# Five full query blocks and packed PV rows in a fused state-space and attention kernel

## The chip, the cores and the metric

The kernel runs on one core of a Trainium2 chip. The metric is device time in microseconds (us) of one execution. The span of a profile, from the first to the last instruction, is about 2 us shorter than the time of that execution. A single core is used, so there is one granted clock of TensorE. Some executions of the kernel before were slow for no reason that the kernel holds (1,502.79 and 804.85 us among the first). Ratios are the mean time of one kernel's fast runs over the mean of the other's fast runs of the same rounds, so they are not quite the ratio of the medians that I quote.

## The reference, cut to what matters

Two independent halves share the core, and their outputs stand side by side.

```python
# A: a diagonal complex state-space model, S = 2048 steps, D = 640 channels
h = Lam_bar * h + Bu[t]                      # a scan over time for each channel
y = 2 * Re(C h) + x * Dskip

# B: attention with 32 heads of Dh = 20, one key and one value head for all
q = (x @ wq)  -> 32 heads x 2048 x 20;  k = x @ wk (2048 x 20);  v = x @ wv (2048 x 20)
p = softmax(q k^T / sqrt(20))                # 32 x 2048 x 2048 exponentials
out = concat_heads(p v) @ wo                 # 640 x 640
```

The exponentials are the bulk: 2,048 tiles of 128 keys x 512 queries (4 query blocks x 32 heads x 16 key blocks).

## The kernel before

The kernel is a generator. A small scheduler in Python simulates the engines with a duration for each step, decides an order for each engine, and emits that order with semaphores. **So the order and the number of instructions of each engine are fixed before the chip starts.** What is left to the chip is how long each instruction takes and how long each engine waits at each semaphore. The steps that matter:

```python
CHUNKS = (3, 2)     # ScalarE takes score tiles in chunks of 3 and 2: 1,536 and 1,024 columns of PSUM
NPS = 7             # buffers (PR) that hold the exponentials until the PV matmuls have read them
NDS = 18            # buffers (DR) of the tiles whose exponential VectorE and GpSimd make with integer steps

def fill(self, op, i):                      # score matmuls of one chunk, then its exponential
    ...
    ex = self.act(lambda e: e.activation(dst, t[:, 0:512 * n], ACT.Exp, scale=1.0 / UNIT), ...,
                  gate=lambda: not h.taken or (h.left == 0 and self.s.done(h.users)))
                  # h: a PR buffer. It is free when all PV matmuls that read it are done
```

A head has 20 rows, and this kernel lets each head start at a multiple of 32 partitions. So four heads are padded to 4 x 32 = 128 partitions, and 32 heads need eight groups. Queries are made in that padded form with 32 matmul columns for 20 useful ones. So are PV, the normalisation and the output projection:

```python
self.WO4 = sb(o, "WO4", [128, NGG, 640], BF16)    # NGG = 8 padded groups
self.OT  = self.sb(s, "OT", [128, 10, 512], BF16) # normalised PV, padded
self.rdB = sb(o, "rdB", [128, 2, 512], BF16)

def queries(self, qb, gg, bank, prev, deps, whole):        # 8 groups x 5 chunks x 4 quarters a query block
    for c in range(NC):                                    # NC = 5
        for j in range(4):
            lhs = p.wqf[:, 640*c + 80*gg + 20*j : ... + 32]
            fns.append(self.mm(bank.tensor[32*j:32*j+32, ...], lhs, p.xbT[:, c, 512*qb:512*qb+512], ...))

def normalize(self, b, ev):                                # after the PV result of head group b is in pvsb
    # denominators to DRAM and back as 64 x 32, reciprocal, to DRAM, then read back on all rows of rdB by DMA
    self.norm_op[b] = self.dve(self.tt(p.OT[:, ot, :], p.pvsb[:, slot, :], p.rdB[:, slot, :], ALU.mult), ...)

def o_task(self, qb, k, bank):
    for gg in range(NGG):                                  # 8 steps of accumulation
        ... self.mm(out, p.OT[:, ots[gg], 128*ts:128*ts+128], p.WO4[:, gg, ...], ...)
```

At the head of the program, sine and cosine tables are made: GpSimd and VectorE reduce the angles, ScalarE applies the sine, then it loads the exponential's table. The first attention exponential comes after that.

Of the kernel before, what the change touches and what calls it, by code (L numbers as in the profile page):

```python
# [402 lines left out]
LIFT = 40.0 * UNIT  # L403


class Build:
    CHUNKS = (3, 2)
    MISC = 2
    NPS = 7
# [17 lines left out]
    def build(self):  # L427
        nc = self.nc
        with ExitStack() as o:
# [22 lines left out]
            with ExitStack() as p2:  # L452
                self.alloc_late(p2)
                late = base - nc.sbuf_bytes_remaining
                if late < early:
                    self.sb(p2, "pad", [128, (early - late) // 4 + 8], FP32)
                self.program()
                self.s.run()
                shares = {k: self.EARLY for k in self.LATE}
                shares.update({f"W{c}_1": [f"xbT{i}_{k}" for i in range(2) for k in range(NC)] for c in range(NC)})  # L460
                shares.update({k: ["xn0", "xn1"] for k in ("CT0", "CT1")})
                em = Emitter(nc, self.s.order, [b.key for b in self.banks], shares)
                em.plan()
                with nc.Block() as block:
                    em.emit(block)

    def alloc(self, o):
# [16 lines left out]
        self.WO4 = sb(o, "WO4", [128, NGG, 640], BF16)  # L484
# [7 lines left out]
        self.aq = sb(o, "aq", [128, 4, 512], BF16)  # L492
# [4 lines left out]
        self.Mm = sb(o, "Mm", [128, NGG, 32], BF16)  # L497
# [9 lines left out]
        self.rdB = sb(o, "rdB", [128, 2, 512], BF16)  # L507
# [9 lines left out]
    def alloc_early(self, s):  # L517
        self.maskM = self.sb(s, "maskM", [128, NGG, 32], FP32)
# [5 lines left out]
        self.EARLY = ["iota", "early_fr00", "early_fr01", "early_fr10", "early_fr11", "vrow", "maskM", "ones32", "mask0"]  # L524

    def alloc_late(self, s):
        self.W = self.sb(s, "W", [128, NC, 2, 512], BF16)
        self.g = self.sb(s, "g", [128, 2, 2, 512], BF16)
        self.OT = self.sb(s, "OT", [128, 10, 512], BF16)
        self.LATE = [f"W{c}_0" for c in range(NC)] + [f"g{u}_{i}" for u in range(2) for i in range(2)] \  # L530
            + [f"OT{i}" for i in range(10)]
# [67 lines left out]
    def program(self):  # L599
# [4 lines left out]
        self.qt_op, self.row_op = {}, {}  # L604
        self.vp_op, self.kt_op, self.vs_op = {}, {}, {}
        self.tasks = []
        self.evac_op, self.norm_op, self.spread_op = {}, {}, {}
        self.o_ops, self.y_ops, self.w_op, self.xa_op = {}, {}, {}, {}
# [63 lines left out]
    def constants(self):  # L672
# [14 lines left out]
        def select(t, pattern, op, v, base, mult, dur):  # L687
# [14 lines left out]
        many("mask0", [fill(p.mask0[:], -1.02, 200),  # L702
# [4 lines left out]
        many("maskM", [fill(p.maskM[:], -1.02, 300),  # L707
                       select(p.maskM[:], [[1, 8], [0, 4], [-1, 8]], ALU.is_equal, 0.0, 0, 0, 650),
                       select(p.maskM[:], [[0, 8], [-32, 4], [0, 8]], ALU.is_ge, 0.0, 0, 1, 650),
                       select(p.maskM[:], [[0, 8], [32, 4], [0, 8]], ALU.is_ge, 0.0, 19, -1, 650)])  # L710
# [10 lines left out]
        self.c_op["WO4"] = self.dve(lambda e: e.memset(p.WO4[:], 0.0), 1500, writes=["WO4"], prio=2.5,  # L721
                                    gate=lambda: self.tile_n > 128)
# [3 lines left out]
    def loads(self):  # L726
# [13 lines left out]
        for c in range(NC):  # L740
# [6 lines left out]
        o = self.loadT([(p.xaT[:, c, :], xa[0, 0:1024, 128 * c:128 * c + 128]) for c in range(NC)], 780000, "xa0", issue=1930.0,  # L747
                       writes=["xaT0", "xaT1"])
        self.xa_op[0] = self.xa_op[1] = o
        self.bt_op = [self.loadT([(p.BT[:, ri, cd, :], src[:, 128 * cd:128 * cd + 128]) for cd in range(NC)], 819200,  # L750
                                 f"bt{ri}", writes=[f"BT{ri}"]) for ri, src in ((0, self.B_re), (1, self.B_im))]
        self.ct_op = [self.loadT([(p.CT[:, ri, cd, :], src[:, 128 * cd:128 * cd + 128]) for cd in range(NC)], 819200,
                                 f"ct{ri}", writes=[f"CT{ri}"]) for ri, src in ((0, self.C_re), (1, self.C_im))]
        wov = self.wo.rearrange("(gg jr) n -> jr gg n", jr=80)
        fns = [lambda e, j=j: e.dma_start(p.WO4[32 * j:32 * j + 20, :, :], wov[20 * j:20 * j + 20, :, :])
               for j in range(4)]
        self.wo_op = self.dma(fns, 819200, "wo", reads=["WO4"], writes=["WO4"], deps=[self.c_op["WO4"]])
# [5 lines left out]
    def xa_load(self, tb):  # L763
        p = self
        self.xa_op[tb] = self.loadT([(p.xaT[:, c, 512 * (tb % 2):512 * (tb % 2) + 512],
                                      self.A_x[0, 512 * tb:512 * tb + 512, 128 * c:128 * c + 128]) for c in range(NC)],
                                    655360, f"xa{tb}", writes=[f"xaT{tb % 2}"])
# [7 lines left out]
    def kv_steps(self):  # L775
# [65 lines left out]
        def bound():  # L841
# [6 lines left out]
            self.mm_op = self.dve(self.ts(p.Mm[:], p.maskM[:], p.mab[:, 4:5], None, ALU.mult), 250,  # L848
                                  deps=[m, self.c_op["maskM"]], reads=["mabs", "maskM"], writes=["Mm"], prio=0.5)
# [67 lines left out]
    def qt_task(self, qb, gg, bank):  # L917
        p = self
        prev = None
        slot = (8 * qb + gg) % 12  # L920
        prev = self.queries(qb, gg, bank, None, [self.wqa_op if gg == 0 else self.wq_op] + bank.last, True)
        dst = p.QT[:, slot, :]
        key = f"QT{slot}"
        first = (qb, gg) == (0, 0)
        if first:
            ev = self.act(lambda e: e.activation(dst, bank.ap, ACT.Copy), 600, deps=[prev], reads=[bank.key],
                          writes=[key], prio=0.3)
        else:
            ev = self.dve(lambda e: e.tensor_copy(dst, bank.ap), 600, deps=[prev], reads=[bank.key], writes=[key],  # L929
                          prio=self.EV)  # L930
        aq = self.dve(self.ts(p.aq[:, gg % 4, :].bitcast(I16), dst.bitcast(I16), 0x7FFF, None, ALU.bitwise_and), 270,
                      deps=[ev], reads=[key], port=True,
                      writes=[f"aq{gg % 4}"], prio=0.4 if first else 2, gate=lambda: self.aq_free(qb, gg))
        self.qt_op[(qb, gg)] = (ev, aq)
        if qb == 0 and gg == 0:
            prev = self.queries(qb, gg, bank, prev, [ev, self.wq0_op], False)
            yield lambda: self.mm_op is not None
            m = self.pe([self.mm(bank.tensor[32 * j:32 * j + 32, bank.off:bank.off + 512], p.M0[:, j, :], p.aq[:, 0, :], False,
                                 True, tile_position=(0, 32 * j), skip_group_check=True) for j in range(4)], self.mmt(512),
                        deps=[self.m0_op, aq], prev=prev, prio=0.5, mode="C", reads=["M0", "aq0", key],  # L940
                        writes=[bank.key])
            ev = self.dve(self.ts(dst, bank.ap, p.lift[:, 0:1], p.lift[:, 1:2], ALU.add, ALU.min), 720,
                          deps=[m, self.lift_op], reads=[bank.key, "lift"], writes=[key, "QTr0"], prio=0.4)
            self.row_op[(0, -1)] = ev
# [4 lines left out]
    def aq_free(self, qb, gg):  # L949
        n = qb * NGG + gg  # L950
        if n < 4:
            return True
        w = self.row_mm.get((n // 4) - 1)
        return w is not None and self.s.done([w])

    row_mm = {}

    def row_task(self, qb, half, bank):
        p = self
        ggs = range(4 * half, 4 * half + 4)  # L960
        prev = None
        rs = (2 * qb + half) % 2
        deps = [self.mm_op] + [self.qt_op[(qb, gg)][1] for gg in ggs] + bank.last
        for gg in ggs:
            prev = self.pe([self.mm(bank.tensor[0:32, bank.off:bank.off + 512], p.Mm[:, gg, :], p.aq[:, gg % 4, :],
                                    gg == ggs[0], gg == ggs[-1])], self.mmt(512), load=128.0, deps=deps, prev=prev,
                           prio=1.5, reads=["Mm", f"aq{gg % 4}"], writes=[bank.key])
        self.row_mm[2 * qb + half] = prev
        ev = self.dve(self.ts(p.brow[:, rs, :], bank.tensor[0:32, bank.off:bank.off + 512], LIFT, 0.0, ALU.add,
                              ALU.min), 620, deps=[prev], reads=[bank.key], writes=[f"brow{rs}"], prio=0.7)  # L970
        lo, ng = 4 * half, 4
        if qb == 0 and half == 0:
            lo, ng = 1, 3
        at = (8 * qb + lo) % 12
        fns = [lambda e, j=j: e.dma_start(p.QT[32 * j + 20:32 * j + 21, at:at + ng, :],
                                          p.brow[8 * j + lo:8 * j + lo + ng, rs, :]) for j in range(4)]
        self.row_op[(qb, half)] = self.dma(fns, 32768, f"row{rs}",
                                           deps=[ev] + [self.qt_op[(qb, gg)][0] for gg in ggs],
                                           reads=[f"brow{rs}"] + [f"QT{i}" for i in range(at, at + ng)],
                                           writes=[f"QTr{i}" for i in range(at, at + ng)], prio=0, land=500.0)  # L980
# [5 lines left out]
    def block_ready(self, b):  # L986
        qb, gg = divmod(b, NGG)
        return self.row_key(b) in self.row_op and (qb, gg) in self.qt_op

    @staticmethod  # L990
    def row_key(b):
# [902 lines left out]
```

## Time and profile before

| | value |
|---|---|
| fast runs, first rounds | 783.91 and 781.43 us; later rounds had medians of 782.2 to 783.2 us |
| span | 781.1 us |
| first exponential starts | 25.6 us (head) |
| last exponential ends | 769.46 us, so the stream is 743.8 us long |
| exponentials busy / ScalarE idle inside the stream | 735.0 / 8.8 us |
| from there to the end | 11.6 us (tail) |

The span is head + busy + idle + tail: 25.6 + 735.0 + 8.8 + 11.6 = 781.1 (rounded terms).

First the page's head (part 1): the span, then busy time, share of the span and instruction count of each engine.

```profile
span 781.1 us, 24633 instructions
...
PE 733.0 (94%) x10668; PEld 247.9 (32%) x10668; DVE 667.5 (85%) x1228; ACT 751.6 (96%) x674; POOL 439.2 (56%) x451
...
```

ScalarE (ACT) is at 96%, TensorE (PE) at 94%. The Trainium skill, "Perfetto Trace Analysis", section "Identifying the Most-Contended Engine", says that busy time is a fair measure of how close ScalarE is to its limit, and that matmul busy time is not one for TensorE.

Next the groups of instructions, by shape. After the names come the count, then busy us in total, mean ns of one, then idle time just before them and what ended it. (Means overlap, so busy is less than count times mean.)

```profile
...
L1079 ACT ACTIVATE PR<-SC 128x1536 bf16<-128x1536 f32 x324 | 505.8, 1561 | 8.0 <-PE MB L581 4.2 <-PE SC L581 3.5
...
L1079 ACT ACTIVATE PR<-SC 128x1024 bf16<-128x1024 f32 x324 | 369.1, 1139 | 2.4 <-PE MB L581 2.4
L596 DVE TENSOR_SCALAR DR<-MB 128x512 int16<-128x512 f32 x428 | 285.4, 684 | 61.5 <-PE MB L581 56.7
...
L581 PE MATMUL MB<-xbT,wqf 128*32 128x512 bf16 x640 | 46.5, 385 | 1.3 <-DVE xbT L797 0.6 <-ACT xbT L800 0.5 <-DVE DR L596 0.2
...
L577 PE MATMUL MB<-WO,OT 128*32 128x512 bf16 x416 | 30.9, 381 | 0.0
...
L577 PE MATMUL MB<-WO,OT 128*32 128x128 bf16 x512 | 11.0, 220 | 0.0
...
L577 PE MATMUL SC<-WO,OT 128*32 128x512 bf16 x96 | 5.8, 379 | 0.0
...
```

The first two lines are the stream: 324 pairs, and their busy times together, counted without overlap, are 735.0 us on the page, so 2.27 us a pair. The third line is the 428 tiles that VectorE takes in place of ScalarE. The last four are what the change reduces: queries (46.5 us) and output projection (30.9 + 11.0 + 5.8 = 47.7 us).

The timeline of ScalarE (start us, duration us, what, count; idle before it in brackets), first and last rows of the stream:

```profile
...
25.62 2.37 ACT L1079 ACTIVATE PR<-SC 128x1536 bf16<-128x1536 f32 x2 [1.55 <-PE SC L581]
...
754.68 14.78 ACT L1079 ACTIVATE PR<-SC 128x1024 bf16<-128x1024 f32 x13
...
```

25.62 is where the stream starts, 754.68 + 14.78 = 769.46 where it ends. What ScalarE's exponentials waited for (us in total, times, longest):

```profile
...
ACT PR L1079 <- PE MB L581: 6.5, 7, 1.5
...
ACT PR L1079 <- PE SC L581: 3.5, 4, 1.5
...
```

The second of these is a wait for scores (SC); the first is a wait for PV matmuls (MB, the PV bank) to finish. 1.55 us of the scores' wait is before the first exponential.

### The profile page before, as it was taken

Reading aid. Unit: us, or ns where it says so; the run is one execution under the profiler, and the core shown is the slowest. Engines: PE = TensorE matmul, PEld = TensorE weight load, DVE = VectorE, ACT = ScalarE, POOL = GpSimd, SP = SyncE. Lnnn points to the kernel's source line nnn. Section 1 sums busy time; section 2 is a strip of 40 time slices with the busy share of each in tenths; the row PEclk is TensorE's granted clock in tenths of the full one; section 3 lists DMA queues with packets and bytes.
Section 4 is the critical chain, followed back from the end, with each engine's and each line's share of the span. In section 5 each row is a group of like instructions: output and inputs, shape, how many; then the busy total and the mean of one; then the engine's idle time right before and its main releaser. Section 6 shows DMA issues by size and latency. Waiting matters only on the chain.

```text
span 781.1 us, 24633 instructions
## 1 busy us (share of the span) xinstructions
PE 733.0 (94%) x10668; PEld 247.9 (32%) x10668; DVE 667.5 (85%) x1228; ACT 751.6 (96%) x674; POOL 439.2 (56%) x451
## 2 busy tenths in 40 slices
PE   8998999999999899999998999999899999999998
PEld 3322222222233333322322332323222333233324
DVE  7899898889988888899998787898889888885985
ACT  5899999999999999999999999999999999999994
POOL 3365655535556445664246645657665575676771
PEclk9999999999999999999999999999999999999999
DMA  9850100000000000011000000110000000001001
GB/s 195 131 96 22 38 9 5 8 8 9 9 9 9 24 16 22 23 25 33 17 16 9 24 30 17 29 30 17 9 11 8 23 30 15 22 11 33 12 9 43
DMA packets 54187, 21.61 MB, mean 28 GB/s; under 512 B 43464, under 2 KB 54080, under 8 KB 54080
## 3 DMA queue, kind: packets, MB, share of 16 engines
q1 hardware_dynamic: 52748, 19.90, 11.8%
q8 instruction: 84, 1.38, 0.7%
q10 hardware_dynamic: 1332, 0.15, 0.1%
q14 instruction: 23, 0.19, 0.1%
HBM read 7.20 MB, written 5.50 MB: 16 GB/s over the span
## 4 chain that ended last, share of the span: by engine, by line
ACT 76%; PE 18%; DVE 3%; POOL 1%; DMA 1%; issue 1%; ACTq 0%; POOLq 0%; DVEq 0%
ACT PR L1079 75%; PE MB L581 7%; PE SC L581 6%; PE MB L577 5%; DVE DR L596 1%; DMA wqf<-in_B_wq_dram 1%; POOL DR L591 1%; PE SC L577 1%; DVE prod L591 0%; DVE WO L721 0%; DVE pvsb L1348 0%; DVE prod L595 0%; DVE Z L1590 0%; DVE Z L1597 0%; DVE QT L929 0%
## 5 line engine op out<-in xcount | busy, mean ns | idle before, releaser
L1079 ACT ACTIVATE PR<-SC 128x1536 bf16<-128x1536 f32 (+1 forms) x648 | 735.0, 1350 | 10.4 <-PE MB L581 6.5
L591 POOL TENSOR_TENSOR DR<-DR,step 128x512 int32<-128x512 int32 x414 | 424.1, 1046 | 308.5 <-DVE DR L596 129.7
L596 DVE TENSOR_SCALAR DR<-MB 128x512 int16<-128x512 f32 x428 | 285.4, 684 | 61.5 <-PE MB L581 56.7
L581 PE MATMUL SC<-QT,KT 32*128 32x512 bf16 x1620 | 252.7, 384 | 35.1 <-ACT PR L1079 25.7
L581 PE MATMUL MB<-DR,VS 128*32 128x512 bf16 x1712 | 233.9, 386 | 3.0 <-DVE pvsb L1348 1.1
L581 PE MATMUL MB<-PR,VP 128*32 128x512 bf16 x1620 | 218.9, 385 | 0.9 <-ACT PR L1079 0.5
L581 PE MATMUL MB<-QT,KT 32*128 32x512 bf16 x428 | 156.5, 385 | 0.9 <-DVE DR L596 0.6
L581 PEld LDWEIGHTS SC<-QT,KT 32*128 32x128 bf16 x1620 | 64.2, 91 | 265.6 <-ACT PR L1079 168.4
L596 DVE TENSOR_SCALAR DR<-DR 128x1024 int16<-128x1024 int16 (+1 forms) x248 | 92.7, 425 | 6.5 <-PE MB L581 4.5
L581 PEld LDWEIGHTS MB<-DR,VS 128*32 128x32 bf16 x1712 | 57.5, 94 | 69.5 <-issue 37.0
L581 PEld LDWEIGHTS MB<-PR,VP 128*32 128x32 bf16 x1620 | 55.1, 94 | 63.7 <-issue 45.8
L577 PE MATMUL MB<-xaT,BT 128*32 128x512 bf16 x800 | 59.3, 382 | 0.0
L591 DVE TENSOR_TENSOR prod<-MB,Z 128x1024 bf16<-128x1024 f32 x40 | 48.7, 1216 | 7.7 <-PE MB L577 7.4
L581 PE MATMUL MB<-xbT,wqf 128*32 128x512 bf16 x640 | 46.5, 385 | 1.3 <-DVE xbT L797 0.6
L581 PE MATMUL MB<-KT,VZ 128*32 128x256 bf16 x844 | 43.7, 275 | 0.0
L581 PEld LDWEIGHTS MB<-QT,KT 32*128 32x128 bf16 x428 | 36.7, 91 | 20.3 <-issue 11.7
L577 PE MATMUL MB<-WO,OT 128*32 128x128 bf16 (+1 forms) x928 | 40.6, 292 | 0.0
L1652 DVE TENSOR_TENSOR_SCAN g<-sc,hst,u 128x512 bf16<-128x512 f32 x30 | 40.4, 1348 | 0.0
L591 DVE TENSOR_TENSOR prod<-g,tab 128x1024 bf16<-128x1024 bf16 x40 | 34.9, 872 | 0.0
L1469 DVE CAST stg<-MB 128x512 bf16<-128x512 f32 x35 | 24.0, 687 | 9.2 <-PE MB L577 8.9
L577 PE MATMUL MB<-CT,W 128*32 128x512 bf16 (+1 forms) x640 | 29.0, 300 | 1.5 <-issue 1.5
L577 PE MATMUL MB<-CT,xbT 128*32 128x512 bf16 (+1 forms) x640 | 29.4, 300 | 0.0
(126 smaller groups left out, 391.7 us busy)
## 6 DMA issues: line engine op xcount, KB each, us to landing
out_dram<-stg SPq DMA_DIRECT2D x35, 128.0 KB, 1.8
rdB<-recs SPq DMA_DIRECT2D x124, 32.0 KB, 1.8
CT<-in_B_x_dram SPq DMA_DIRECT2D x2, 640.0 KB, 5.8
WO<-in_B_wo_dram SPq DMA_DIRECT2D x4, 200.0 KB
wqf<-in_B_wq_dram SPq DMA_DIRECT2D x1, 680.0 KB, 5.2
out_dram<-PR SPq DMA_DIRECT2D x5, 128.0 KB, 1.8
sums<-pvsb SPq DMA_DIRECT2D x31, 4.0 KB
dn<-sums SPq DMA_DIRECT2D x31, 4.0 KB, 1.8
```

What stands on the lines that cost most here:

```text
L577: r = e.matmul(out[32 * j:32 * j + 32], lhsT=lhsT[:, 32 * j:32 * j + 32], rhs=rhs, start=start, stop=stop, tile_position=(0, 32 * j), skip ...
L581: return lambda e: e.matmul(out, lhsT=lhsT, rhs=rhs, start=start, stop=stop, **kw)
L591: return lambda e: e.tensor_tensor(out, a, b, op)
L596: return lambda e: e.tensor_scalar(out, a, s1, s2, op0=op0, op1=op1)
L1079: ex = self.act(lambda e: e.activation(dst, t[:, 0:512 * n], ACT.Exp, scale=1.0 / UNIT), 0.8333 * 512 * n + 64, table="exp", deps=[op], re ...
L1469: ev = self.dve(lambda e: e.tensor_copy(st, bank.ap), 620, deps=[prev], reads=[bank.key], writes=[key], prio=self.EV, gate=(lambda: last.e ...
L1652: o = self.dve(lambda e, ri=ri, init=init: e.tensor_tensor_scan(p.g[:, u, ri, :], rdec, p.u[:, ri, :], init, ALU.mult, ALU.add), 1280, por ...
```

## The change

Intent: do not pad where padding is not needed. Queries are made as five full blocks of 128 rows, written to DRAM, and read back into the padded rows by DMA. PV results are sent by DMA from padded to packed rows; the reciprocal is spread by DMA in the packed form too; normalisation and projection then need five blocks instead of eight groups. That frees TensorE and VectorE and costs DMA issues. The core of the diff:

```diff
-    NPS = 7
+    NPS = 8
+    NOP = 7
+    NRD = 3
...
-        self.WO4 = sb(o, "WO4", [128, NGG, 640], BF16)
+        self.WO = sb(o, "WO", [128, NC, 640], BF16)
+        self.WOt = sb(o, "WOt", [128, 640], BF16)
-        self.aq = sb(o, "aq", [128, 4, 512], BF16)
+        self.QP = sb(o, "QP", [128, NC, 512], BF16)
-        self.rdB = sb(o, "rdB", [128, 2, 512], BF16)
+        self.rdP = sb(o, "rdP", [128, self.NRD, 512], BF16)
-        self.OT = self.sb(s, "OT", [128, 10, 512], BF16)
+        self.OP = self.sb(s, "OP", [128, self.NOP, 512], BF16)
...                                               # the padding rows of the query tile, once, in the head
+        many("QTz", [("pool", lambda e, i=i: e.memset(p.QT[:, i:i + 2, :], 0.0), 600) for i in (1, 3, 5, 7, 9)]
+             + [("pool", lambda e: e.memset(p.QT[:, 11, :], 0.0), 330)], "QTz")
...                                               # queries: a full block, out to DRAM
+    def q_task(self, qb, blk, bank):
+        for c in range(NC):
+            at = 640 * c + 128 * blk
+            prev = self.pe([self.mm(bank.ap, p.wqf[:, at:at + 128], p.xbT[:, c, 512 * qb:512 * qb + 512], ...)])
+        ev = self.dve(lambda e: e.tensor_copy(dst, bank.ap), 600, ...)
+        out = self.dma(lambda e: e.dma_start(rows, dst), 131072, f"qd{blk}", deps=[ev], ...)
...                                               # and back into the heads' padded rows
+            fns = [lambda e, ...: e.dma_start(p.QT[32 * j:32 * j + 20, at:at + ng, :], q[j][:, lo:lo + ng, :])
+                   for j in range(4)]
...                                               # PV result to packed rows, reciprocal likewise, then one multiply
+            fns = [lambda e, ...: e.dma_start(p.OP[to:to + n, at, :], p.pvsb[32 * j + d:32 * j + d + n, slot, :])
+                   for j, d, to, n in parts]
+            fns = [lambda e, ...: e.dma_start(p.rdP[to:to + n, rd, :], recs[j:j + 1, :].to_broadcast([n, 512]))
+                   for j, d, to, n in parts]
+                    self.tt(p.OP[0:rows, at, :], p.OP[0:rows, at, :], p.rdP[0:rows, rd, :], ALU.mult), 350, ...
...                                               # projection: five steps (six for the last query block)
+        for blk in range(NC):
+            steps.append((NC * qb + blk, p.OP[:, at, :], p.WO[:, blk, :], [f"OP{at}", "WO"]))
+        if last:
+            steps.append((NC * NQB, p.pvsb[:, slot, :], p.WOt[:], [f"pvsb{slot}", "WOt"]))
```

Cut: the bound on the scores (a row that keeps the exponential in range) is computed for full blocks as well; loads of one half are issued in smaller pieces. Bytes a partition, by the shapes above: 2,560 less in the weights, 3,072 less in the PV results, 1,024 more for the reciprocals (4,608 less), and 3,072 more for an eighth buffer for exponentials, 3 x 512 columns of bf16.

## The prediction

> **What bounds it now.** The span is 781.1 us. ScalarE is the pace: the page gives it 96% busy, and the chain of waits runs through its exponentials for 75%. Groups by shape: 324 exponentials of 1,536 and 324 of 1,024 columns, 735.0 us together, so 2.27 us a pair (0.454 us a score tile), with 10.4 us idle before them, part of it at the start. The timeline has the first at 25.6 us and the last ending at about 769.5: 25.6 head + 735 + 9 idle + 11.6 tail. The other 428 of 2,048 score tiles get their exponential on VectorE; TensorE is 94% busy, VectorE 85%, the DMA engines nearly idle after 60 us.
>
> **What the change does**, from instruction counts of both programs:
> - TensorE: query matmuls 640 to 420 (46.5 us before, so about -16), output projection 1,024 to 672 (47.7, about -16), bound rows 32 to 20 (-3.6): 36 us freed.
> - VectorE: query evictions 31 to 20 (0.684 us each), absolute values 32 to 21 (0.30), normalisations 32 to 21 (0.49), bound-row evictions 8 to 4, no 2.2 us memset: 21 us freed.
> - DMA issues on the sync queue 341 to 550 at about 0.5 us: some 105 us more of a queue that mostly waits.
> - Six more GpSimd memsets before the start.
>
> **How much is critical.** Freed TensorE and VectorE time does not shorten ScalarE's stream; only fewer tiles on ScalarE do. The program moves just 15: exponentials on VectorE 428 to 443, ScalarE's 648 to 642. That is 3 pairs, 6.8 us. Most freed time is spent again: 15 first evictions (10 us), more shifted copies (about 11), 60 more PV matmuls (8). ScalarE's stream goes from 735.0 to about 728.2 us.
>
> Head: VectorE range-reduction steps now stand behind the third max-reduction, and memsets between GpSimd's table steps; I expect the first exponential 1 us later (26.6). The second head block waits for query and bound rows by DMA after 55 ScalarE tiles, at 51 to 52 us. By durations of before, evictions, absolute values and bound row end near 47; then query rows and bound rows are issued, landing near 51 to 52. I expect a stall of 0 to 3 us there, 1 in the middle. Later query blocks come hundreds of tiles ahead. The Trainium skill, "DMA: Bandwidth & Descriptors", "Rules for kernel authors", says to issue a DMA early and wait late, so that its fixed cost overlaps; this trace's 1.8 us to landing agrees with a cost that can hide. In-order coupling of sync queue and VectorE (absolute values in place wait for the query write): 2 us more idle.
>
> Tail: the last projection has six steps instead of eight, about -1 us.
>
> Sum: 26.6 + 728.2 + 9 + 1 + 2 + 10.7 = 777.5 us span; with the 2 us between span and time, 779.5. Against the fast time of before, 783.91, that is -0.6%: within 2%. (The median 804.85 holds slow runs.) Range 770 to 797; chances 0.14 faster, 0.79 same, 0.07 slower.
>
> **What shows it.** Exponentials about 728 us; the first at 26 to 27.5 us; query and projection matmuls about 30 us each; ScalarE's idle 10 to 15 us, the largest gap near 51 us, for query rows; DMA share under 0.2 after 60 us; tail 10 to 11 us.
>
> **What would make it wrong.** The in-order sync queue holding scatters or query reads behind a wait, so that evictions and then ScalarE stall in every block (slower). Or freed TensorE time removing most of ScalarE's idle (a few us faster). Over 2% faster needs nearly no idle: 26 + 728 + 10 is 764 already.

## More of the kernel before

Last a detail of the head, from VectorE's timeline. It looked harmless: five small steps of 128 x 5 elements.

```profile
...
12.50 0.99 DVE L595 TENSOR_SCALAR trig<-sc 128x5 f32<-128x5 f32 x5 [0.23 <-POOL fr L596]
...
```

They take 0.99 us together.

## The result, and the profile after

Four runs of the changed kernel gave 771.84 to 774.01 us, median 772.62. The ratio to before is 0.9874, 95% interval 0.9838 to 0.9909. A second set (below) gave the same median and 0.9863 (0.984 to 0.9886). So it is faster by 1.3 to 1.4%, which is within 2%. It lies inside the predicted range, but the predicted gain was 0.6%. Page, groups, timeline and waits, in the order of before:

```profile
span 770.8 us, 23905 instructions
...
PE 718.7 (93%) x10155; PEld 240.9 (31%) x10158; DVE 668.6 (87%) x1235; ACT 743.6 (96%) x668; POOL 438.8 (57%) x453
...
```

```profile
...
L1142 ACT ACTIVATE PR<-SC 128x1536 bf16<-128x1536 f32 x321 | 510.5, 1590 | 3.8 <-PE MB L587 1.9 <-PE SC L587 1.8
...
L1142 ACT ACTIVATE PR<-SC 128x1024 bf16<-128x1024 f32 x321 | 375.4, 1169 | 0.4 <-PE MB L587 0.2 <-PE SC L587 0.2
L602 DVE TENSOR_SCALAR DR<-MB 128x512 int16<-128x512 f32 x443 | 294.5, 684 | 60.1 <-PE MB L587 54.8 <-POOL DR L597 0.2
...
L583 PE MATMUL MB<-xbT,wqf 128*32 128x512 bf16 x400 | 28.7, 390 | 0.0
...
L583 PE MATMUL MB<-WO,OP 128*32 128x512 bf16 x260 | 20.8, 382 | 0.0
...
L583 PE MATMUL MB<-WO,OP 128*32 128x128 bf16 x320 | 6.8, 220 | 0.0
...
L583 PE MATMUL SC<-WO,OP 128*32 128x512 bf16 x60 | 4.3, 379 | 0.0
...
```

```profile
...
29.43 4.75 ACT L1142 ACTIVATE PR<-SC 128x1536 bf16<-128x1536 f32 x4 [0.55 <-PE SC L587]
35.42 19.75 ACT L1142 ACTIVATE PR<-SC 128x1536 bf16<-128x1536 f32 x17 [1.24 <-PE SC L587]
55.35 5.54 ACT L1142 ACTIVATE PR<-SC 128x1024 bf16<-128x1024 f32 x5 [0.17 <-PE SC L587]
...
743.96 16.06 ACT L1142 ACTIVATE PR<-SC 128x1536 bf16<-128x1536 f32 x14
...
```

```profile
...
ACT PR L1142 <- PE MB L587: 2.0, 4, 1.5
ACT PR L1142 <- PE SC L587: 2.0, 3, 1.2
...
```

TensorE's work fell as counted: queries 46.5 to 28.7 us (this line has 400 of 420), projection 47.7 to 20.8 + 6.8 + 4.3 = 31.9, and 1.8 more in 32 matmuls of the last query block's sixth step. VectorE took 443 tiles instead of 428 and is as busy as before (668.6 against 667.5). The stream has 321 pairs. It starts at 29.43 us and ends at 743.96 + 16.06 = 760.02. ScalarE's waits for PV fell from 6.5 to 2.0 us.

| term, us | before | predicted | after | change |
|---|---|---|---|---|
| head | 25.6 | 26.6 | 29.4 | +3.8 |
| exponentials busy (648 / 642 / 642) | 735.0 | 728.2 | 726.9 | -8.1 |
| ScalarE idle in the stream | 8.8 | 12 | 3.7 | -5.1 |
| tail | 11.6 | 10.7 | 10.8 | -0.9 |
| span | 781.1 | 777.5 | 770.8 | -10.3 |

Two terms were mis-sized, in opposite directions: the head and the idle. The head first. In VectorE's timeline of the changed kernel, the small steps are small no more:

```profile
...
7.64 1.69 DVE L602 TENSOR_SCALAR sc<-sc 128x5 f32<-128x5 f32 x1
...
14.10 3.10 DVE L601 TENSOR_SCALAR trig<-sc 128x5 f32<-128x5 f32 x4 [0.24 <-POOL fr L602]
...
20.38 0.16 DVE L597 TENSOR_TENSOR sc<-sc,trig 128x5 f32<-128x5 f32 x1 [1.08 <-POOL fr L602]
20.58 0.68 DVE L601 TENSOR_SCALAR sc<-sc 128x5 f32<-128x5 f32 x1
...
```

Four of the five 128 x 5 steps now take 3.10 us. In GpSimd's timeline of the same time:

```profile
...
7.47 0.94 POOL L694 TENSOR_SCALAR_AFFINE_SELECT pick<-pick 20x640 f32<-20x640 f32 x1 [2.98 <-DVE sc L1597]
8.36 0.94 POOL L718 MEMSET QT<- 128x1024 bf16 x1
...
14.01 2.97 POOL L718 MEMSET QT<- 128x1024 bf16 x3
...
20.29 0.95 POOL L718 MEMSET QT<- 128x1024 bf16 x1
...
```

Three memsets of the query tile run from 14.01 to 16.98 us, just while three of those steps crawl, about one memset long each. The earlier step at 7.64 us (1.69 us) overlaps the mask step and the first memset in the same way. Under the memset at 20.29 us a two-input step (`tensor_tensor`) still took 0.16 us, and the one-input `tensor_scalar` step after it 0.68 us. So it is the `tensor_scalar` steps that suffer. The Trainium skill has this: "SBUF — State Buffer", section "Who interferes with whom", says that GpSimd and VectorE's two-port modes share one pair of ports, that it is an exclusive lock held for the whole instruction, and that `tensor_scalar` can enter those modes. I had not carried it over to steps of five elements.

Last the windows view of the changed kernel: length, then busy us and instructions of each engine (PE, PEld, DVE, ACT, POOL), then granted clock, DMA share and GB/s.

```profile
...
28.00:52.00 24.00, 23.03 (x322) 9.02 (x326) 21.00 (x49) 22.09 (x21) 11.84 (x19) 0.86 0.46 95
52.00:100.00 48.00, 45.38 (x593) 14.64 (x595) 43.67 (x81) 47.83 (x43) 28.44 (x29) 1.00 0.36 78
100.00:200.00 100.00, 91.62 (x1127) 28.46 (x1119) 91.47 (x170) 100.00 (x90) 55.36 (x55) 1.00 0.07 19
...
```

The DMA engines are not idle after 60 us, as I had said: their share is 0.36 from 52 to 100 us (0.39 from 60 to 100), where it was 0.18 before; from 100 us on it is about 0.1. No wait of ScalarE can be read from it; the only idle near the start of the second head block is the 0.17 us at 55.35 us in the timeline above. The clock of 0.86 in the first row is a stretch of 6.8 us at half clock, from 28.7 us on; see the next section.

### The profile page after: what moved, and what is told of

It reads as the page before. It is cut to its first block, busy times and chain, and to the rows that moved or that the text cites. A ratio compares the mean times of both kernels' runs of the same rounds, so it can differ in the third digit from the quotient of the medians.

```text
span 770.8 us, 23905 instructions
## 1 busy us (share of the span) xinstructions
PE 718.7 (93%) x10155; PEld 240.9 (31%) x10158; DVE 668.6 (87%) x1235; ACT 743.6 (96%) x668; POOL 438.8 (57%) x453
## 4 chain that ended last, share of the span: by engine, by line
ACT 82%; PE 13%; DVE 3%; DMA 1%; POOL 0%; issue 0%; ACTq 0%; SPq 0%; POOLq 0%
ACT PR L1142 82%; PE MB L583 5%; PE MB L587 4%; PE SC L587 4%; DMA wkr<-in_B_wk_dram 1%; PE SC L583 1%; DVE DR L602 1%; DVE trig L601 0%; POOL fr L602 0%; DMA xaT<-in_A_x_dram 0%; DVE fr L602 0%; ACT tab L1647 0%; DVE sc L602 0%; PE MB L936 0%; DVE sc L1597 0%
## 5 line engine op out<-in xcount | busy, mean ns | idle before, releaser
L1142 ACT ACTIVATE PR<-SC 128x1536 bf16<-128x1536 f32 (+1 forms) x642 | 726.9, 1380 | 4.3 <-PE MB L587 2.0
L597 POOL TENSOR_TENSOR DR<-DR,step 128x512 int32<-128x512 int32 x410 | 418.3, 1044 | 301.3 <-DVE DR L602 128.5
L602 DVE TENSOR_SCALAR DR<-MB 128x512 int16<-128x512 f32 x443 | 294.5, 684 | 60.1 <-PE MB L587 54.8
L587 PE MATMUL MB<-DR,VS 128*32 128x512 bf16 x1772 | 225.9, 385 | 0.7 <-DVE DR L602 0.3
L587 PE MATMUL MB<-QT,KT 32*128 32x512 bf16 x443 | 162.8, 384 | 0.6 <-DVE DR L602 0.4
L602 DVE TENSOR_SCALAR DR<-DR 128x1024 int16<-128x1024 int16 (+1 forms) x275 | 101.6, 423 | 6.6 <-PE MB L587 4.8
L587 PE MATMUL MB<-KT,VZ 128*32 128x256 bf16 x860 | 45.5, 275 | 0.0
L1750 DVE TENSOR_TENSOR_SCAN g<-sc,hst,u 128x512 bf16<-128x512 f32 x30 | 42.3, 1415 | 0.0
L583 PE MATMUL MB<-xbT,wqf 128*32 128x512 bf16 x400 | 28.7, 390 | 0.0
L583 PE MATMUL MB<-WO,OP 128*32 128x128 bf16 (+1 forms) x580 | 27.1, 292 | 0.0
```

The source lines that it names most:

```text
L583: r = e.matmul(out[32 * j:32 * j + 32], lhsT=lhsT[:, 32 * j:32 * j + 32], rhs=rhs, start=start, stop=stop, tile_position=(0, 32 * j), skip ...
L587: return lambda e: e.matmul(out, lhsT=lhsT, rhs=rhs, start=start, stop=stop, **kw)
L597: return lambda e: e.tensor_tensor(out, a, b, op)
L602: return lambda e: e.tensor_scalar(out, a, s1, s2, op0=op0, op1=op1)
L1750: o = self.dve(lambda e, ri=ri, init=init: e.tensor_tensor_scan(p.g[:, u, ri, :], rdec, p.u[:, ri, :], init, ALU.mult, ALU.add), 1280, por ...
```

## The experiments

Every build goes through the scheduler again, so a small edit reorders the whole program. The count of exponentials is known before the run. Idle and tail still move by a microsecond or two from order alone, and I do not read differences of that size as effects. Fast medians of the kernel before in e1 to e4, e5 to e8, e9 to e11 and e12 were 782.8, 782.9, 782.2 and 783.2 us.

| run | exponentials | head | busy | idle | tail | span | median time | ratio to before |
|---|---|---|---|---|---|---|---|---|
| before | 648 | 25.6 | 735.0 | 8.8 | 11.6 | 781.1 | 782.8 | |
| after | 642 | 29.4 | 726.9 | 3.7 | 10.8 | 770.8 | 772.6 | 0.9874 |
| e1 late memsets | 643 | 24.8 | 728.7 | 3.8 | 11.5 | 768.8 | 770.9 | 0.9852 |
| e2 seven buffers | 643 | 29.5 | 728.1 | 5.8 | 11.6 | 774.9 | 776.3 | 0.9928 |
| e3 query half, seven buffers | 645 | 29.3 | 730.9 | 5.5 | 11.9 | 777.5 | 780.2 | 0.9968 |
| e4 output half, seven buffers | 646 | 25.4 | 731.7 | 9.2 | 11.2 | 777.5 | 779.1 | 0.995 |
| e5 before + memsets | 648 | 29.5 | 734.8 | 7.2 | 11.7 | 783.2 | 785.5 | 1.0042 |
| e6 after, 428 tiles on VectorE | 648 | 29.4 | 733.5 | 4.1 | 10.4 | 777.4 | 779.9 | 0.9974 |
| e7 output half, eight buffers | 646 | 25.8 | 730.6 | 3.7 | 10.0 | 770.2 | 771.1 | 0.985 |
| e8 late memsets, margin 500 | 640 | 24.9 | 725.8 | 8.0 | 11.2 | 769.8 | 773.4 | 0.9887 |
| e9 before, eight buffers | 650 | 25.6 | 737.3 | 6.8 | 11.9 | 781.6 | 781.7 | 0.9986 |
| e10 late memsets, ahead 8 | 642 | 25.2 | 727.2 | 6.7 | 12.9 | 772.0 | 773.9 | 0.989 |
| e11 e8 with nine buffers | 643 | 24.8 | 728.2 | 3.5 | 13.0 | 769.4 | 770.8 | 0.9851 |
| e12 after, unaltered | 642 | 28.9 | 726.8 | 4.4 | 10.8 | 771.0 | 772.6 | 0.9863 |

Head, idle and tail are read as for before and after: first and last exponential from ScalarE's timeline, busy from the groups. The terms come from rounded rows and can be 0.1 us off. (e7, e8, e10 and e11 have one more exponential than was counted ahead, for a single left-over tile.) The rows "after" and e12 are one program on two occasions: 0.5 us of head and 0.7 us of idle lie between them.

**One thing besides the order seems to move the idle: the clock.** In every profile the granted TensorE clock falls to half for one or more stretches (of 3.4, 6.8 or 10.2 us where they begin before the stream ends), and some of ScalarE's gaps fall into them. Before: 76.4 to 79.8 us, with 1.1 of its 8.8 us of idle in it or just after it. e4: 502.5 to 505.9 us (`prof e4_o_only --windows 502.5:505.9` gives a clock of 0.50), with a single gap of 2.3 us. e9: 29.6 to 33.0 and 149.1 to 152.5 us, with 2.6 us. e10: among others 512.4 to 515.8 us, with 1.5 us. e7 has none inside the stream. Most of the others have theirs in the first microseconds of the stream, where a gap can also come from the order. Times go with it: the four runs of e8 took 771.5, 771.8, 775.0 and 777.2 us at mean clocks of 0.997, 0.997, 0.991 and 0.984. Why the clock falls, and why elsewhere in another order, no run shows; nor does any run fix the clock, so that a gap comes from it is argued from place and time. So idle is compared below with these stretches in mind, and times at equal clock where there are such runs.

### Late memsets (e1)

My theory of the head: GpSimd's memsets hold up VectorE's small steps. Rival: the new order of VectorE and TensorE is to blame. The edit moves the memsets behind the start of the stream:

```diff
-        many("QTz", [("pool", lambda e, i=i: e.memset(p.QT[:, i:i + 2, :], 0.0), 600) for i in (1, 3, 5, 7, 9)] + ..., "QTz")
+        for i, n in ((1, 2), (3, 2), (5, 2), (7, 2), (9, 2), (11, 1)):
+            prev = self.s.add("pool", lambda e, i=i, n=n: e.memset(p.QT[:, i:i + n, :], 0.0), 300 * n, ...,
+                              gate=lambda: self.started)
```

> The changed kernel with one part moved: the six GpSimd memsets that clear the padded query tile run after the exponentials have started instead of among the range-reduction steps of the head. The program has 643 exponentials on ScalarE (the changed kernel 642). Theory A (the head grew by 3.8 us, 25.6 to 29.4 us to the first exponential, because VectorE's small steps are held up while a GpSimd memset of 0.95 us runs): the four small trig steps take about 0.2 us each again instead of 3.1 us together, the first exponential starts at 25.5 to 26.8 us, and the time is 769 to 771 us (772.6, plus 1.1 for one exponential more, less 3 to 4), unless ScalarE now waits 1 to 3 us for query rows near 51 us. Rival B (the head grew because the new program orders VectorE and TensorE differently): the first exponential stays at 28.5 us or later and the time is 772.5 to 774.5 us.

The first exponential, from ScalarE's timeline:

```profile
...
24.84 4.62 ACT L1146 ACTIVATE PR<-SC 128x1536 bf16<-128x1536 f32 x4 [0.68 <-PE SC L587]
...
```

and VectorE's trig steps, from the groups (count, busy us, mean ns):

```profile
...
L601 DVE TENSOR_SCALAR trig<-sc 128x5 f32<-128x5 f32 x5 | 0.8, 169 | 0.5 <-POOL fr L602 0.5
...
```

Both are back, the head at 24.8 us, even 0.8 earlier than before the change. Time: 770.94 us, 1.7 less than the changed kernel though the head is 4.6 shorter; the span of the profiles differs by 2.0. The rest went to one exponential more (busy +1.8) and to the tail (+0.7). A head that starts earlier did not lead to a stall for query rows: its profile has no gap over 0.1 us on ScalarE between 38 and 95 us.

### The memsets alone, added to the kernel before (e5)

```diff
+        many("DUM", [("pool", lambda e, i=i: e.memset(p.stg[:, i:i + 2, :], 0.0), 600) for i in (0, 2, 0, 2, 0)]
+             + [("pool", lambda e: e.memset(p.stg[:, 2, :], 0.0), 330)], "DUM")
```

(One more line, not shown, keeps the first real use of that tile behind the memsets.)

> The kernel before with the suspected cost alone added: six GpSimd memsets of the same sizes (five of 128 x 1,024, one of 128 x 512, bf16), into a staging tile that is unused until later, in the same place of the head. ScalarE keeps its 648 exponentials. Theory A (these memsets hold up VectorE's small steps and so the head): VectorE's trig steps take about 0.6 us each on average instead of 0.17, the first exponential moves from 25.6 to 28.5 to 29.5 us, and the time grows by 3 to 4 us to 785.5 to 787 us. Rival B (the head grew for another part of the change): first exponential at 25.6 to 26.5 us, time 782 to 783.5 us.

The same two views, for this run:

```profile
...
L595 DVE TENSOR_SCALAR trig<-sc 128x5 f32<-128x5 f32 x5 | 3.2, 634 | 0.4 <-POOL fr L596 0.2
...
```

```profile
...
29.51 2.36 ACT L1081 ACTIVATE PR<-SC 128x1536 bf16<-128x1536 f32 x2 [2.77 <-PE SC L581]
...
```

The trig steps take 3.2 us instead of 0.9, and the head is 29.5 us, 3.9 more. With e1 that settles the head: the cost goes with the memsets, in either kernel. The time grew by less, 2.6 us by medians (ratio 1.0042, so 3.3 by means), because 1.7 us of idle went away (7.2 us from 8.8), mostly 0.6 at the start of the stream, and 0.9 at 76 to 80 us, where the clock fell to half in the profile of before and not in this one. From 269 us on the two profiles have the same gaps, 2 us apart. The added memsets thus cost the head 3.9 us, in line with theory A.

### Seven buffers in the changed kernel (e2)

Why did the idle fall? Theory A: the eighth buffer. Rival B: TensorE has less other work. One number is edited: `NPS = 8` to `7`.

> The changed kernel with seven buffers for exponentials, as before, instead of eight. The program has 643 exponentials (642), so one ScalarE instruction more, 1.1 us. Theory A (ScalarE's idle among the exponentials fell from 8.8 to 3.7 us because the eighth buffer, which the change added, spares it waits for PV matmuls that still read the oldest): ScalarE's waits for TensorE's PV group are back at 5 to 7 us from 2.0, its idle at 8 to 10 us, the time 776 to 779 us. Rival B (idle fell because TensorE has 36 us less other work): idle stays at 3 to 5 us and the time is 773 to 775 us.

ScalarE's waits:

```profile
...
ACT PR L1142 <- PE MB L587: 3.3, 3, 1.9
...
ACT PR L1142 <- PE SC L587: 3.1, 4, 1.2
...
```

Idle 5.8 us: between the two expectations; the waits for PV, 3.3 us, are short of A's 5 to 7. The time, 776.3 us, is in A's range, 3.7 over the changed kernel, made of 2.1 idle, 1.2 for the exponential, 0.8 tail (the profiled span grew by 4.1). Against the second profile of the changed kernel (e12: idle 4.4, waits for PV 2.6) the buffer is worth 1.4 us of idle. It is part of the reason, not all of it.

### The two halves alone (e3, e4)

Each half was put into a build of its own, with seven buffers. The query half keeps the changed kernel's query steps and takes `normalize`, `norm_task`, `o_task`, the weights and the output tiles of before. The output half is the reverse.

```diff
 # e3: the changed kernel, but
-        self.OP = self.sb(s, "OP", [128, self.NOP, 512], BF16)      # also WO, WOt, rdP, the steps that use them
+        self.OT = self.sb(s, "OT", [128, 10, 512], BF16)            # also WO4, rdB, their steps
-    NPS = 8
+    NPS = 7
 # e4: the kernel before, but
-        self.OT = self.sb(s, "OT", [128, 10, 512], BF16)
+        self.OP = self.sb(s, "OP", [128, self.NOP, 512], BF16)
```

> Only the query half of the change: queries in five blocks of 128 rows over DRAM; normalisation and output projection as before, in eight padded groups; seven buffers for exponentials. The program has 645 exponentials on ScalarE (before 648, changed 642). Theory A (ScalarE's count sets the stream, idle depends on the eighth buffer, and the memsets of the query half cost the head 3.8 us): first exponential at 29 to 30 us, exponentials busy about 730 us, idle 8 to 10 us, time 780 to 783 us, no faster than before at 782. Rival B (freed TensorE time takes the idle away): idle 4 to 6 us and 776 to 779 us.

> Only the output half of the change: PV results sent by DMA to packed rows, projection in five blocks; queries as before in eight padded groups; seven buffers for exponentials. The program has 646 exponentials (before 648, changed 642). Theory A: first exponential at 25.5 to 26 us as before (no memsets of the query tile), exponentials busy about 732 us, idle 8 to 10 us, tail 10.5 to 11 us; time 777.5 to 780 us, 3 us under before. Rival B (freed TensorE time takes the idle away): idle 4 to 6 us and 774 to 776.5 us.

The query half: head 29.3 us, so the memsets came with it, but idle 5.5 us, as the rival said; the time, 780.2 us, is at the lower edge of theory A's range and not in the rival's. The output half's waits, and the gap at half clock in its timeline:

```profile
...
ACT PR L1083 <- PE MB L584: 7.2, 6, 2.3
...
ACT PR L1083 <- PE SC L584: 3.2, 3, 1.5
...
```

```profile
...
506.09 14.58 ACT L1083 ACTIVATE PR<-SC 128x1024 bf16<-128x1024 f32 x13 [2.29 <-PE MB L584]
...
```

Idle 9.2 us, as theory A said; 779.1 us. Without the gap of 2.3 us it is 6.9, against 7.7 of before less its own 1.1. The one run of e4 at full clock took 776.6 us, the three at 0.996 to 0.998 took 779.0 to 779.6. So with seven buffers the idle fell with the query half (to 5.5 us) and hardly with the output half. Query work moved off TensorE is spread over the whole stream, while projection work comes in bursts; whether that is why, no run shows.

### The output half with eight buffers (e7)

> The output half alone, as in the run before, now with eight buffers for exponentials instead of seven. 645 exponentials (646). If the eighth buffer takes 2 us of ScalarE's idle, as between the changed kernel with seven and with eight: idle 6.5 to 8 us from 9.2, time 775 to 777 us from 779.1. If the buffer does nothing and the difference there was chance of the order: idle 8.5 to 10 us, time 777.5 to 779.5 us.

Edit: `NPS = 7` to `8` in the build of e4. Its waits:

```profile
...
ACT PR L1083 <- PE SC L584: 3.4, 2, 1.8
...
ACT PR L1083 <- PE MB L584: 1.7, 2, 1.3
...
```

Waits for PV fell from 7.2 to 1.7 us, idle from 9.2 to 3.7, and the time from 779.1 to 771.1 us, with one tile of difference in VectorE's share (434 against 433). This is more than either expectation allowed. Not all of it is the buffer's: 2.3 us of e4's waits and idle are the gap at half clock, which e7 does not have. That leaves 3.2 us of idle. At full clock the times are 776.6 (one run of e4) and 771.1 and 771.2 us. The output half and the buffer alone reach the time of the whole change.

### The eighth buffer in the kernel before (e9)

The space was found by moving three tiles that only the head uses into the region that is reused later.

```diff
-        self.sel32 = sb(o, "sel32", [32, 128], BF16)               # likewise wq0 and wk4
+        self.sel32 = self.sb(s, "sel32", [32, 128], BF16)          # in the early, reused region
-    NPS = 7
+    NPS = 8
```

> The kernel before with the eighth buffer for exponentials alone (the space found by placing three tiles that only the head uses into the region that is reused later; nothing else changed). The program has 650 exponentials on ScalarE (before 648) and 423 tiles on VectorE (428). If the eighth buffer takes ScalarE's idle by itself (5.5 us between the two runs of the output half): idle 3.5 to 5 us from 8.8, exponentials busy 736 to 738 us, time 778.5 to 781 us, so 2 to 4 us under before. If the buffer only helps where the output half has freed TensorE: idle 7.5 to 9.5 us and 783 to 786 us.

```profile
...
ACT PR L1079 <- PE SC L581: 4.7, 4, 1.5
...
ACT PR L1079 <- PE MB L581: 3.1, 6, 1.1
...
```

Waits for PV halve here too (6.5 to 3.1 us), and waits for scores rise (3.5 to 4.7). Idle is 6.8 us, 2.0 less; the two more exponentials that this order has cost 2.3 us of busy time. By all fast runs there is no change (ratio 0.9986, interval 0.9953 to 1.0019), and neither expectation holds: the idle lies between them, and so does the time. But the profiled run (783.4 us) is one of the two slower ones, at a clock of 0.996, and 2.6 us of its idle lie in two stretches at half clock. The two runs at full clock took 779.9 us each, three of before at full clock 781.8 to 782.2 us. So by itself the eighth buffer is worth 2 us of idle, or up to 3.5 without the stretches of either profile; whether time was won is not settled: about 2 us at full clock, and nothing over all runs.

### The count of exponentials (e6)

```diff
+        if self.d_count + taken + 1 > 428:
+            return False
```

> The changed kernel with VectorE's share of the exponentials held at the 428 tiles of before (changed: 443), so 648 exponentials on ScalarE again. Theory A (the time follows ScalarE's instruction count): exponentials busy 733 to 735 us, idle 3 to 5 us as in the changed kernel, time 6 to 8 us over the changed kernel, 778.5 to 781 us. Rival B (the gain is the freed TensorE time itself and the count matters little): idle falls under 3 us and the time stays at 772 to 775 us.

The page's group of all exponentials, in this run:

```profile
...
L1142 ACT ACTIVATE PR<-SC 128x1536 bf16<-128x1536 f32 (+1 forms) x648 | 733.5, 1389 | 4.4 <-PE MB L587 2.2
...
```

Busy 733.5 us for 648, idle 4.1, time 779.9: 7.3 us over the changed kernel, for six exponentials more. From 264 to 705 us its gaps are those of the changed kernel but for one of 0.18 us, so here the order hardly interferes. The count is the largest single term of the gain, as predicted, and TensorE's freed time did not turn into less idle beyond that.

### Moving more tiles off ScalarE (e8, e10), and a ninth buffer (e11)

If the count sets the time, scheduling constants that lower it should pay. (e11 gets its space by moving two tiles as e9 did.)

```diff
 # e8, on top of e1                  # e10, on top of e1                # e11, on top of e8
-    MARGIN = 650.0                   -    AHEAD = 10                    -    NPS = 8
+    MARGIN = 500.0                   +    AHEAD = 8                     +    NPS = 9
```

> The changed kernel with the late memsets and one scheduling constant changed (the scheduler may wait longer for a free bank before it fills the next score bank: margin 500 instead of 650), which moves four more instructions off ScalarE: 639 exponentials (643 with late memsets alone, 642 in the changed kernel). If the count sets the time: busy 723 to 725 us, first exponential at 24.8 to 25.5 us, idle 3.5 to 6 us, time 766 to 768.5 us. If the smaller margin is paid in ScalarE idle: idle 7 us or more and 769.5 us or more.

> The changed kernel with the late memsets and a scheduling constant (a block is left for the next one's VectorE tiles at 8 remaining tiles instead of 10): 641 exponentials (643 with late memsets alone), 444 tiles on VectorE. If fewer instructions on ScalarE pay: busy 726 us, idle 3.5 to 5 us, 767.5 to 770 us against 770.9. If a tile moved off ScalarE comes back as ScalarE idle, as with the smaller margin (idle 8.0 us there): idle 6 us or more and 770.5 us or more.

> The kernel with the smaller margin and late memsets, with nine buffers for exponentials instead of eight (space as in the run before with the eighth buffer). 642 exponentials, 442 tiles on VectorE. If buffers are what keeps ScalarE from waiting for PV matmuls: its waits for TensorE's PV group fall to under 2.5 us from 4.8 at eight buffers, idle 3 to 5 us from 8.0, time 767.5 to 770.5 us. If those waits come from TensorE's lack of time, whatever the buffers: idle 6.5 us or more and 771 us or more.

e8 has three exponentials less than e1 (640) and won nothing: idle 8.0 us from 3.8, 773.4 us. That median holds the two runs at a low clock; the two at 0.997 took 771.5 and 771.8 us, the two of e1 at 0.997 took 770.4 and 771.0. e10, with one exponential less, did not pay either: idle 6.7 us (1.5 of it at half clock at 512 us), a tail of 13.0 us, 773.9 us at clocks of 0.991 to 0.994; e1's run at 0.994 took 771.5. In e10 the idle is made of both kinds of waits:

```profile
...
ACT PR L1146 <- PE SC L587: 3.5, 4, 1.5
ACT PR L1146 <- PE MB L587: 3.4, 6, 1.3
...
```

With a ninth buffer (e11) the idle is 3.5 us and the waits for PV 1.3 us, as the buffer's theory said, but the order that the scheduler then found has 643 exponentials and a tail of 13.0 us; 770.8 us, equal to e1. So in these orders fewer exponentials came back as idle: busy 2.9 us less and idle 4.2 more in e8, 1.5 less and 2.9 more in e10. That TensorE can no longer serve the stream there is likely but not shown.

### The changed kernel again (e12)

> The changed kernel unaltered, in five rounds against before, because its first interval (0.984 to 0.991) rests on few fast runs of before and overlaps that of the late memsets (0.9835 to 0.987). If the late memsets are worth the 1.7 us that the medians say: ratio 0.9865 to 0.9885, time 771.8 to 773.5 us. If the two are equal: ratio 0.985 to 0.986, time near 771 us.

772.62 us median (772.1 to 773.14), ratio 0.9863 (0.984 to 0.9886). The ratio lies between the two expected bands, just below the first; the time is in the first. The intervals of e1 and of the changed kernel overlap, so by ratio they are not told apart. By times, all runs of e1 (770.43 to 771.49) lie below all of the changed kernel's in both sets (771.84 to 774.01), though not of the same call; at the same clock of 0.994 it is 771.5 against 773.1 and 774.0. e1, e7 and e11 all measured 770.8 to 771.1 us: clearly faster than before by 1.5%, and at best 0.2% faster than the changed kernel.

## Why the prediction was right or wrong, point by point

- **Verdict and range: right.** Within 2%, and 772.6 us lies in 770 to 797. The point, 779.5, was 7 us too high. That it was no further off is luck: the idle was 8.3 us smaller than predicted, and a head 2.8 us longer than predicted hid a third of that.
- **"ScalarE's stream goes from 735.0 to about 728.2 us": right.** Measured 726.9. Holding the count (e6) cost 7.3 us, so the count is shown as the cause of that part.
- **Freed VectorE time is spent again: right.** Its busy time stayed (667.5 and 668.6 us), with first evictions up from 285.4 to 294.5 us.
- **"I expect the first exponential 1 us later (26.6)": mis-sized.** It was 3.8 us later. The prediction counted the memsets as GpSimd's own time; what they cost was VectorE's: its `tensor_scalar` steps lasted as long as the memsets (e1, e5). That they waited for the shared ports is inferred; the runs show the times alone.
- **"A stall of 0 to 3 us", "1 in the middle", for the second head block: not there.** The order needs the rows after 55 ScalarE tiles, and the stream started 3.8 us later, so the need moved as well. With the early head of e1 there was no stall either, so the step was too pessimistic, not only lucky.
- **"2 us more idle" and an unchanged 9: the step that failed most.** Idle was 3.7 instead of 12 us. The step behind it is "Freed TensorE and VectorE time does not shorten ScalarE's stream; only fewer tiles on ScalarE do": the idle inside the stream fell as well. The prediction did not look at the buffer count at all, the first line of the diff. With it undone, idle is 5.8 (e2); the rest of the fall came with the query half (e3: 5.5 with seven buffers). In the output half the same buffer took 5.5 us (e4, e7), 2.3 of them in a stretch at half clock. The warning "freed TensorE time removing most of ScalarE's idle" named the direction, and half of the cause.
- **Tail, "about -1 us": right** (-0.9), though other orders moved it by up to 1.4 us the other way.
- **"DMA share under 0.2 after 60 us": wrong up to 100 us,** 0.39 from 60 to 100 us and about 0.1 after that; it had no visible cost.
- **What each half is worth.** The output half alone, with the buffer for which it makes room, gives 771.1 us. The query half on top makes four exponentials fewer and a head 3.6 us longer, and the whole is 772.6. With its memsets moved it is 770.9. So with eight buffers the query half is worth nothing that these runs can tell from zero (e7 ran at clocks of 0.999 to 1.0, the others at 0.994 to 0.998); with seven it was worth 2.8 us by medians (779.1 to 776.3), which the clocks blur too: e4 at full clock took 776.6.

What stays open: how much of the fall in idle is the buffer's. As profiled it took 5.5 us in the output half and 2 us elsewhere; without the stretches at half clock in mid-stream it is 3.2 us there and about 2 us elsewhere. Each build has its own order and its own stretches at half clock, and no run holds either fixed while the buffer changes.

## What to carry to other kernels

Write the span as head, busy, idle and tail of the pacing engine, and price each term of a change on its own: here +3.8 and -5.1 us hid behind each other. Look at what a smaller layout frees in memory, not only in work: the buffer that it pays for can be worth as much as the matmuls that it saves. Keep GpSimd's long instructions away from chains of small `tensor_scalar` steps on VectorE, above all in the head, where nothing else covers the wait. And before a difference of 1 to 3 us in idle is put down to the program, look at the granted clock inside each gap: a mean of 0.997 held one gap of 2.3 us at half clock.

## What the Trainium skill lacked or had wrong

- "SBUF — State Buffer", section "Who interferes with whom": the lock is stated, and the runs agree. Missing is how it looks for small steps: 128 x 5 `tensor_scalar` steps of 0.17 us took 0.63 us on average next to 0.95 us memsets (e5: 5 steps, 0.9 to 3.2 us busy), and the head grew by 3.9 us.
- "VectorE: DVE Perf Modes", section "Zero memsets can be issued as uint32 (trn2)", speaks of VectorE's memsets. No page gives the time of a GpSimd memset; here 128 x 1,024 bf16 took 0.95 us and 128 x 128 took 0.2 us.
- "Perfetto Trace Analysis", section "Optimization Strategy", says that repeated gaps on the saturated engine can mean too few buffers. The runs agree (waits for PV 6.5 to 3.1 us, 7.2 to 1.7 us, 3.3 to 2.0 us with the eighth buffer). Missing in that section is a look at the granted clock before buffers are counted: 2.3 of the 7.2 us lay in one stretch at half clock.
